# Two FFN2 chunks in the array's 64-row lanes, and two small moves in the start-up of a gated state-space and feed-forward kernel

## The chip, the cores and the metric

The kernel runs on one core of one Trainium2 chip. The metric is the device time of one execution in microseconds (us), taken as the median of several executions. The engines are called as in the profile: PE is TensorE (matmuls), PEld its weight loads, DVE is VectorE, ACT is ScalarE, POOL is GpSimd, SP is SyncE; SPq and ACTq are the places from which DMAs are issued.

## The reference

For one sequence of 2048 rows and 448 features, the output mixes two branches with a gate per row:

```python
g = sigmoid((x * gate_w).sum(-1, keepdims=True))
# a: a diagonal complex state-space model (P = D = 448)
Bu = x @ B_bar.T                       # B_bar from Lambda, log_dt, B
h[t] = Lam_bar * h[t-1] + Bu[t]        # 2048 steps
a = 2 * real(h @ C.T) + x * Dskip
# b: a feed-forward network, w1 448x1792 (FFN1), w2 1792x448 (FFN2)
b = silu(x @ w1) @ w2
out = g * a + (1 - g) * b
```

All inputs and the output are bf16.

## The kernel before

The rows are split into even and odd ones, 1024 each, so that the scan runs over pairs of rows. Each parity has two halves of 512 rows. The feed-forward branch works by chunks: chunk c holds parity `c // 2` and half `c % 2`. Of one chunk, FFN1 makes 14 blocks of 128 hidden features by 512 rows, two blocks at a time; ACT applies silu from PSUM and writes them to the SBUF tile `AT[c % 2]`. FFN2 of the chunk then makes four output tiles of 128 rows by 448 features, each a sum over the 14 hidden blocks in one PSUM bank, and a result step scales the bank and writes it to SBUF. For chunk 0 that step is on DVE (L790), for the others on ACT (L795).

The contraction of FFN1 is 448 = 3.5 x 128 rows. To waste none of the array, FFN1 and the products with B run in **lanes** (L358 to L396): the array's upper and lower 64 rows (`LO`, `UP`) work as two arrays of 64 x 128, each with its own weights and its own bank. `pair` sends blocks e and o through `lanes` in three passes: the first three 128-row blocks with e's lower half and o's upper half, the remainder of 64 rows for both, and a **swapped** pass that gives each bank its other half. The swapped pass is put into `waiting` and is issued by `settle()` after the next pair's first pass, so that PE need not wait: `T.passed("pe", c)` makes PE wait for its own earlier pass before the other lane adds to the same bank. FFN2 (`ffn2`, L770 to L796), the transposes of x and the last stage use the whole array of 128 rows; the last stage multiplies the states by C (L1004), called the output stage here.

All engines run in order. A small tracker (`T.op`) writes the waits from the names that an operation reads and writes. The order of the work is the order in which lines 1057 to 1182 call the pieces; several are generators that `run(g, n)` moves on by n steps: `s0` to `s3` are the scans on DVE, `t0` to `t3` the sine and cosine tables on ACT, `g0` to `g3` the gate and the skip term, `ca` and `cd` the matrices from C on ACT and DVE. PSUM has eight banks. `nxt()` hands out the next one of the list `BANKS`, `skip(n)` passes over n of them, `at(p)` names the pair of banks number p counted from `base`. FFN2 of chunk 0 is at L1102 to L1112, that of chunk 1 at L1136 to L1144; each is followed by FFN1 of the chunk after the next (chunk 2 at L1116, chunk 3 at L1149). FFN2 of chunks 2 and 3 (L1150 to L1164) is not touched.

In the start-up, x of chunk 0 is loaded in pieces (`XH`; the last piece, half of the columns, is `XA[4]`) and transposed on PE (`turn_x`, L487), two transposes for each call; DVE copies them out (`turned_x`, L495). The first six FFN1 blocks (`ffn1_first`, L425) run on the whole array, spread between the transposes by `yield`: six matmuls for each 128-row block j of the contraction. Three parameter rows (`log_dt`, `Lambda_re`, `Lambda_im`) are loaded into `R` (`ld_row`, L261), filled up to 512 columns by a small DVE copy (`rd`, L463), turned into columns by four small matmuls (`mm_cols`, L467) and copied to `PV` by DVE (L513). The transposes of blocks 1 and 3 use the same PSUM bank as these columns, so those of block 3 wait for the copy to `PV`.

Of the kernel before, what the change touches and what calls it, by code (L numbers as in the profile page):

```python
# [19 lines left out]
D = 448  # L20
F_FF = 1792
NFB = 14
# [128 lines left out]
def gated_mix(nc, A_x, A_Lambda_re, A_Lambda_im, A_B_re, A_B_im, A_C_re, A_C_im, A_log_dt,  # L151
              A_Dskip, B_x, B_w1, B_w2, gate_w, out):
    with ExitStack() as ctx:
        E = ctx.enter_context
        T = Tracker(nc, ctx)

        def sb(name, shape, dtype):
            return E(nc.sbuf_tensor(name, list(shape), dtype))
# [6 lines left out]
        W2 = sb("W2", [128, NFB, D], BF16)  # L165
# [11 lines left out]
        AT = [sb(f"AT{i}", [128, NFB, 512], BF16) for i in range(2)]  # L177
# [30 lines left out]
        def bsk(tile):  # L208
            if tile % 2:
                return BTK if tile == 1 else []  # L210
            return {0: ["IOTA"], 8: ["COS0"], 12: ["SIN0"]}.get(tile, [])
# [9 lines left out]
        ps = E(nc.psum_tensor("ps", [128, 8, 512], F32))  # L221
        BANKS = list(range(8))


        def ld(eng, dst, src, key, group=None):
            return T.dma(eng, lambda e: e.dma_start(dst, src), writes=[key], group=group)
# [23 lines left out]
        def row(v):  # L250
            return v.rearrange("(o n) -> o n", o=1)

        XH = XN[:, 0:8 * D].rearrange("p (k c) -> p k c", k=4)
        XA = ["XA0", "XA1", "XA2", "XA3", "XB"]
        FA, FB = 768, 1280
        x0 = x2[0:512, 0:512].rearrange("(k p) c -> p k c", p=128)

        def ld_w(eng, j, f0=0, f1=FA, key=""):
            ld(eng, W1E[:, j, f0:f1], B_w1[j * 128:(j + 1) * 128, f0:f1], f"W1Ej{j}{key}")

        def ld_row(eng, i, v):  # L261
            ld(eng, R[i:i + 1, 0:D], row(v), f"R{i}", gR if i < 2 else gR2)
# [5 lines left out]
        def ld_wr(eng, c, later):  # L268
            p = slice(64 * c, 64 * c + 64)
            if later:  # L270
                return ld(eng, W1E[p, 3, 384:896].rearrange("p (n f) -> p n f", n=2),
                          B_w1[384:448, FA:].rearrange("p (n c f) -> p n c f", n=2, c=2)[:, :, c, :], f"W1Es{c}")
            return ld(eng, W1E[p, 3, 0:384], B_w1[384:448, 384 * c:384 * c + 384], f"W1Er{c}")
# [5 lines left out]
        for k, eng in ((2, "sp"), (3, "act")):  # L279
            ld(eng, XH[:, k, 0:256], x0[:, k, 0:256], XA[k])  # L280
        ld_w("sp", 1)
        ld("act", XH[:, :, 256:512], x0[:, :, 256:512], XA[4])
        for i, (eng, v) in enumerate((("sp", A_log_dt), ("sp", A_Lambda_re), ("act", A_Lambda_im))):
            ld_row(eng, i, v)
        ld_w("sp", 2)
        gE = [ld_wr(eng, c, False) for c, eng in enumerate(("sp", "act"))]
        ld_w3("sp", 0, 2, FA, FB, "d")
# [21 lines left out]
        for i, src in enumerate((A_B_re, A_B_im)):  # L309
# [15 lines left out]
            base=0, channel_multiplier=1), reads=["ID"], writes=["ID"])  # L325
        T.op("pool", lambda e: e.iota(IOTA[:, :].bitcast(I32), pattern=[[1, NK]], base=0, channel_multiplier=0),
             writes=["IOTA"])
# [7 lines left out]
        n_bank = [0]  # L335

        def nxt():
            n_bank[0] += 1
            return BANKS[(n_bank[0] - 1) % len(BANKS)]

        LO, UP = slice(0, 64), slice(64, 128)
# [10 lines left out]
        def settle():  # L352
            while waiting:
                b, after = waiting.pop(0)
                b()
                after()
# [41 lines left out]
        def ff(fb):  # L398
            i, c = fb // 2, fb % 2
            return i + 3 * c if i < 3 else i + 3 + 2 * c if i < 5 else i + 5 + 2 * c  # L400
# [12 lines left out]
        base = [0]  # L413

        def at(p):
            return [BANKS[(base[0] + 2 * p + i) % len(BANKS)] for i in range(2)]
# [8 lines left out]
        def ffn1_first():  # L425
            banks = [nxt() for _ in range(NF1)]
            for j, h in ((0, 0), (0, 1), (1, None), (2, None)):
                c = slice(0, 512) if h is None else slice(256 * h, 256 * h + 256)
                for n, fb in enumerate((0, 2, 4, 1, 3, 5)):
                    bank = banks[fb]  # L430
                    T.op("pe", lambda pe, fb=fb, bank=bank, j=j, h=h, c=c: pe.matmul(  # L431
                        ps[:, bank, c], W1E[:, j, ff(fb) * 128:(ff(fb) + 1) * 128], XT[:, j, c],
                        start=(h == 0), stop=(h == 0), skip_group_check=(h != 0)),
                        reads=[f"W1Ej{j}" if j else f"W1Ej0{fb % 2}"] + (
                            ["XTe02"] if j == 2 else [f"XTe0{j}{h}"] if h is not None else [f"XTe0{j}0", f"XTe0{j}1"]),
                        writes=[f"ps{bank}"])
                    if (j, h, n) in ((0, 0, 3), (0, 0, 5), (1, None, 2)):
                        yield
            yield banks

# [46 lines left out]
        def turn_x(j, i):  # L487
            def mm(pe):
                ins = None
                for k in (2 * i, 2 * i + 1):  # L490
                    ins = pe.transpose(xp[j][:, k * 128:(k + 1) * 128], XH[:, k, j * 128:(j + 1) * 128], ID[:, :])  # L491
                return ins
            T.op("pe", mm, reads=(XA[2 * i:2 * i + 2] if j < 2 else [XA[4]]) + ["ID"], writes=[f"ps{PB[j]}"])

        def turned_x(j, i=None):  # L495
            c, key = (slice(0, 512), f"XTe0{j}") if i is None else (slice(256 * i, 256 * i + 256), f"XTe0{j}{i}")
            T.op("dve", lambda e: e.tensor_copy(XT[:, j, c], xp[j][:, c]), reads=[f"ps{PB[j]}"], writes=[key])

        for j in range(2):
# [3 lines left out]
        first = ffn1_first()  # L503
# [9 lines left out]
        T.op("dve", lambda e: e.tensor_copy(  # L513
            PV[:, :, :], ps[:, 7, 256:288].rearrange("p (t c) -> p t c", c=8)[:, :, 0:4]),
            reads=["pv", "ps7"], writes=["PV"])
        for j in (2, 3):
            for i in range(2):
                turn_x(j, i)
        turned_x(2)

        names = {}

# [21 lines left out]
        def pact(o, a, f, ra, scale=1.0, bias=0.0):  # L544
# [20 lines left out]
            reads=["f2"] + SGN, writes=["f2s"])  # L565
        first = next(first)
# [59 lines left out]
        def block(tile):  # L626
            return tile // 4 if tile > 7 else tile % 2
# [10 lines left out]
        def skip():  # L638
            for b in range(4):
                v, ks = xblock(b)  # L640
                T.op("dve", lambda e, v=v: e.tensor_tensor(
                    v, v, DB[:, :].unsqueeze(1).to_broadcast([128, 4, D]), ALU.mult),
                    reads=ks + ["DB"], writes=[f"XD{b}"] + ks)
                yield
# [12 lines left out]
             writes=["BTz"] + BTK[2:4])  # L657
# [7 lines left out]
        W2K = ["W20", "W21"]  # L665
# [95 lines left out]
        def xd(tile):  # L761
            return XN[:, tile * D:(tile + 1) * D]
# [5 lines left out]
                 reads=[f"XD{block(tile)}", "GRO"], writes=[f"ps{bank}"])  # L768

        def ffn2(c, q):  # L770
            odd, h = c // 2, c % 2
            kt = 4 * h + q
            tile = 2 * kt + odd
            a = AT[c % 2]
            first = c != 2
            settle()
            bank = nxt()

            def mm(pe):
                ins = None  # L780
                for fb in range(NFB):
                    ins = pe.matmul(ps[:, bank, 0:D], a[:, fb, q * 128:(q + 1) * 128], W2[:, ff(fb), :],  # L782
                                    start=(first and fb == 0), stop=(fb == NFB - 1),
                                    skip_group_check=not first)
                return ins
            T.op("pe", mm, reads=[f"AT{c % 2}_{fb}" for fb in range(NFB)] + W2K,
                 writes=[f"ps{bank}"])
            ks = [f"BS{tile}"] + bsk(tile)
            if c == 0:
                T.op("dve", lambda e: e.scalar_tensor_tensor(  # L790
                    bs(tile), ps[:, bank, 0:D], GT[:, 3, tile:tile + 1], xd(tile), ALU.mult, ALU.add),
                    reads=[f"ps{bank}", "GRI", f"XD{block(tile)}"], writes=ks)
                return
            sc = GT[:, 3, tile:tile + 1] if h == 0 else GT[:, 2, tile:tile + 1]
            T.op("act", lambda e: e.activation(bs(tile), ps[:, bank, 0:D], AF.Copy, scale=sc),  # L795
                 reads=[f"ps{bank}", "GT2" if h else "GRI"], writes=ks)  # L796
# [213 lines left out]
        def yopen():  # L1010
            return yhalf(YA, *seeds.pop(0))
# [30 lines left out]
        def run(g, n=10 ** 9):  # L1042
            for _ in range(n):
                if next(g, "end") == "end":
                    break

        coef = side_coef()
        ca, cd = c_act(), c_dve()
# [50 lines left out]
        settle()  # L1099
        run(g3, 1)  # L1100
        run(s1, 1)
        n_bank[0] = base[0] + 6  # L1102
        run(g1)
        ffn2(0, 0)
        run(s0, 1)
        ffn2(0, 1)
        run(t3)
        run(g2, 4)
        ffn2(0, 2)
        run(g2)  # L1110
        run(g3)
        ffn2(0, 3)  # L1112
        run(s0, 1)
        run(s3, 1)
        run(g0)
        f = ffn1(2)  # L1116
# [16 lines left out]
        run(s0)  # L1133
        run(s3)
        run(s1, 5)
        ffn2(1, 0)  # L1136
        run(t2)
        ffn2(1, 1)
        run(ca, 4)
        skip(4)  # L1140
        ffn2(1, 2)
        run(ca)
        ffn2(1, 3)
        skip(2)  # L1144
        run(cd)
        run(s2, 2)
        run(s1)
# [17 lines left out]
        for _ in range(8):  # L1165
            t = yclose(*yopen())
# [4 lines left out]
        kt, odd = tiles[-1]  # L1171
# [6 lines left out]
        for c in (slice(0, 280), slice(280, D)):  # L1178
            kt, odd, bank = seeds.pop(0)
# [37 lines left out]
```

## Time and profile before

| | |
|---|---|
| median of 3 runs | 137.66 us (137.56 to 137.89) |
| the profiled execution | 137.38 us |
| its span, first to last instruction | 136.1 us |
| PE busy | 133.1 us, 98% of the span |
| DVE busy | 113.9 us, 84% |
| ACT busy | 93.9 us, 69% |
| granted TensorE clock | 1.000 |

The page lists the busy time of each engine, the chain of work that ended last (followed back from the last instruction), and the costliest groups of instructions by line. The timeline lists instructions in order of time; neighbours of the same line, engine and shape are merged into one row with their count, and the length of a row reaches to the end of its last instruction. A matmul's own length (some 0.35 to 0.38 us here) includes the way through the array, and the next one starts before it ends; the rate is read from the starts. Times are us from the start of the span unless marked ns. A few matmul records are missing from the trace.

### The profile page before, as it was taken

Reading aid. Unit: us, or ns where it says so; the run is one execution under the profiler, and the core shown is the slowest. Engines: PE = TensorE matmul, PEld = TensorE weight load, DVE = VectorE, ACT = ScalarE, POOL = GpSimd, SP = SyncE. Lnnn points to the kernel's source line nnn. Section 1 sums busy time; section 2 is a strip of 40 time slices with the busy share of each in tenths; the row PEclk is TensorE's granted clock in tenths of the full one; section 3 lists DMA queues with packets and bytes.
Section 4 is the critical chain, followed back from the end, with each engine's and each line's share of the span. In section 5 each row is a group of like instructions: output and inputs, shape, how many; then the busy total and the mean of one; then the engine's idle time right before and its main releaser. Section 6 shows DMA issues by size and latency. Waiting matters only on the chain.

```text
span 136.1 us, 2407 instructions
## 1 busy us (share of the span) xinstructions
PE 133.1 (98%) x962; PEld 66.3 (49%) x963; DVE 113.9 (84%) x150; ACT 93.9 (69%) x146; POOL 16.9 (12%) x32
## 2 busy tenths in 40 slices
PE   7999999999999999999999999999999999999993
PEld 7744444444444554444445544445555555555552
DVE  1377999375699999999999999999999999991554
ACT  0458888899939999778996996797213436879300
POOL 7109669314000000000000000000000000000000
PEclk9999999999999999999999999999999999999999
DMA  4998949999999230000311000000000000222123
GB/s 111 261 288 163 161 99 169 183 145 367 299 205 198 55 92 0 5 0 0 76 43 39 0 0 0 0 5 0 0 0 0 0 5 0 101 84 85 67 79 124
DMA packets 24911, 11.94 MB, mean 88 GB/s; under 512 B 16579, under 2 KB 24390, under 8 KB 24902
## 3 DMA queue, kind: packets, MB, share of 16 engines
q1 hardware_dynamic: 23156, 10.76, 35.4%
q10 hardware_dynamic: 1746, 1.04, 2.7%
q8 instruction: 7, 0.11, 0.3%
q14 instruction: 2, 0.02, 0.0%
HBM read 5.51 MB, written 1.84 MB: 54 GB/s over the span
## 4 chain that ended last, share of the span: by engine, by line
PE 97%; DVE 1%; issue 0%
PE ps L363 43%; PE ps L782 31%; PE ps L1004 15%; PE ps L431 4%; PE ps L479 2%; PE ps L491 1%; DVE TMPS L1028 1%; PE ps L445 1%; PE ps L470 0%
## 5 line engine op out<-in xcount | busy, mean ns | idle before, releaser
L782 PE MATMUL ps<-W,AT 128*128 128x448 bf16 x224 | 42.9, 353 | 0.0
L363 PE MATMUL ps<-XT,W1E 64*128 64x512 bf16 x325 | 41.4, 376 | 0.0
L453 ACT ACTIVATE AT<-ps 128x1024 bf16<-128x1024 f32 x28 | 28.2, 1019 | 8.1 <-PE ps L363 7.6
L782 PEld LDWEIGHTS ps<-W,AT 128*128 128x128 bf16 x224 | 21.7, 98 | 21.2 <-ACT CO L733 0.4
L363 PEld LDWEIGHTS ps<-XT,W1E 64*128 64x128 bf16 x325 | 16.7, 94 | 19.4 <-issue 0.4
L363 PE MATMUL ps<-XT,BT 64*128 64x512 bf16 x156 | 22.4, 376 | 0.0
L795 ACT ACTIVATE BT<-ps,GT 128x448 bf16<-128x448 f32 x8 | 5.1, 633 | 13.2 <-PE ps L782 13.2
L363 PEld LDWEIGHTS ps<-XT,BT 64*128 64x128 bf16 x156 | 8.1, 94 | 9.3 <-DVE HS L851 0.3
L895 DVE TENSOR_TENSOR_SCAN G<-P,Q 128x1024 f32<-128x1024 f32 (+1 forms) x6 | 11.4, 1920 | 0.0
L1004 PE MATMUL ps<-CO,VE 128*128 128x448 bf16 (+2 forms) x63 | 11.1, 332 | 0.0
L1004 PE MATMUL ps<-CO,HS 128*128 128x448 bf16 x56 | 11.1, 352 | 0.0
L851 DVE SCALAR_TENSOR_TENSOR HS<-VE,P,ps 128x512 bf16<-128x512 bf16 (+1 forms) x13 | 9.6, 779 | 1.7 <-PE ps L363 1.6
L363 PE MATMUL ps<-XR,W1E 64*128 64x512 bf16 x25 | 9.2, 376 | 0.0
L1004 PEld LDWEIGHTS ps<-CO,VE 128*128 128x128 bf16 x63 | 6.0, 98 | 4.8
L1004 PEld LDWEIGHTS ps<-CO,HS 128*128 128x128 bf16 x56 | 5.5, 98 | 5.1
L848 DVE TENSOR_TENSOR Q<-G,COS 128x2048 bf16<-128x2048 f32 (+1 forms) x4 | 7.0, 1756 | 0.1
L848 DVE TENSOR_TENSOR Q<-G,SIN 128x2048 bf16<-128x2048 f32 (+1 forms) x4 | 7.0, 1750 | 0.0
L813 ACT ACTIVATE VE<-ps 128x1024 bf16<-128x1024 f32 x6 | 6.1, 1019 | 1.2 <-PE ps L363 1.2
L815 ACT ACTIVATE ps<-VE,P 128x1024 f32<-128x1024 bf16 x6 | 6.7, 1118 | 0.2
L851 DVE SCALAR_TENSOR_TENSOR VE<-HS,P,FP 128x512 bf16<-128x512 bf16 (+1 forms) x7 | 6.6, 977 | 0.1
L1028 DVE SCALAR_TENSOR_TENSOR OT<-ps,GT,BT 128x448 bf16<-128x448 f32 x4 | 2.6, 681 | 4.7 <-PE ps L1004 4.7
L851 DVE SCALAR_TENSOR_TENSOR FP<-HS,P,VE 128x1024 f32<-128x1024 bf16 (+1 forms) x4 | 6.2, 1550 | 0.1
(120 smaller groups left out, 173.8 us busy)
## 6 DMA issues: line engine op xcount, KB each, us to landing
W<-in_B_w_dram SPq DMA_DIRECT2D x2, 784.0 KB, 8.1
XN<-in_A_x_dram SPq DMA_DIRECT2D x1, 896.0 KB, 6.5
out_dram<-OT SPq DMA_DIRECT2D x8, 112.0 KB, 1.7
out_dram<-TMPS SPq DMA_DIRECT2D x7, 112.0 KB, 1.7
HS<-HS SPq DMA_DIRECT2D x4, 128.0 KB, 2.5
W1E<-in_B_w_dram SPq DMA_DIRECT2D x2, 192.0 KB, 4.0
XN<-in_A_x_dram SPq DMA_DIRECT2D x1, 384.0 KB, 5.8
XN<-in_A_x_dram ACTq DMA_DIRECT2D x1, 256.0 KB, 4.6
```

What stands on the lines that cost most here:

```text
L363: ins = pe.matmul(ps[:, bank, :], w(p, j), xh(odd, h, j, p), start=start and j == js[0], stop=stop and j == js[-1], skip_group_check=seeded)
L431: T.op("pe", lambda pe, fb=fb, bank=bank, j=j, h=h, c=c: pe.matmul(ps[:, bank, c], W1E[:, j, ff(fb) * 128:(ff(fb) + 1) * 128], XT[:, j, c] ...
L453: T.op("act", lambda e: e.activation(a[:, fb:fb + n, :], ps[:, bank:bank + n, :], AF.Silu), reads=[f"ps{bank + i}" for i in range(n)], wri ...
L782: ins = pe.matmul(ps[:, bank, 0:D], a[:, fb, q * 128:(q + 1) * 128], W2[:, ff(fb), :], start=(first and fb == 0), stop=(fb == NFB - 1), sk ...
L795: T.op("act", lambda e: e.activation(bs(tile), ps[:, bank, 0:D], AF.Copy, scale=sc), reads=[f"ps{bank}", "GT2" if h else "GRI"], writes=ks)
L813: T.op("act", lambda e: e.activation(VE[:, m:m + 2, hs], ps[:, b[0]:b[0] + 2, :], AF.Copy), reads=[f"ps{i}" for i in b], writes=vs)
L815: T.op("act", lambda e: e.activation(ps[:, o[0]:o[0] + 2, :], VE[:, m:m + 2, hs], AF.Copy, scale=c1("lr", pt)), reads=vs + ["lr"], writes= ...
L848: T.op("dve", lambda e: e.tensor_tensor(o, a, b, op), reads=reads, writes=writes)
L851: T.op("dve", lambda e: e.scalar_tensor_tensor(o, a, s, b, ALU.mult, ALU.add), reads=reads, writes=writes)
L895: T.op("dve", lambda e: e.tensor_tensor_scan(G[:, c, w], rb, Q1[:, c, w], init, ALU.mult, ALU.add), reads=[f"Q1{c}", "rr", f"G{c}"], write ...
L1004: ins = pe.matmul(ps[:, bank, c], state(kt, odd, m), CO[:, m, c], start=False, stop=(m == YB[-1]), skip_group_check=True)
L1028: T.op("dve", lambda e: e.scalar_tensor_tensor(o, ps[:, bank, c], g, bs(tile)[:, c], ALU.mult, ALU.add), reads=[f"ps{bank}", "GT1_1", f"BS ...
```

## The change

Three edits.

1. FFN2 of chunks 0 and 1 no longer uses the whole array. `ffn2_all(c)` takes the four tiles as two couples. `ffn2_lanes` runs one pass of 14 x 2 matmuls of 64 rows by 448 columns: the lower lane adds to one tile's bank, the upper lane to the other's. First the first pass of both couples, then the swapped pass of both; before a swapped pass PE waits for the end of the same couple's first pass. The result steps move into `ffn2_out`, unchanged in themselves, and are called in two groups of two. So the order on DVE (chunk 0) and on ACT (chunk 1) changes: the second scan step comes ahead of chunk 0's first result, and table `t2` and three steps of `ca` come ahead of chunk 1's first two results. For chunk 0 the bank list is rearranged.
2. The DMA of the third parameter row (`Lambda_im`, on ACT's queue) is issued before the last piece of x instead of after it.
3. The first six FFN1 blocks get a further `yield`, and the three matmuls before it are put between the transposes of x's block 2 and those of block 3.

```diff
@@ loads
-        ld("act", XH[:, :, 256:512], x0[:, :, 256:512], XA[4])
         for i, (eng, v) in enumerate((("sp", A_log_dt), ("sp", A_Lambda_re), ("act", A_Lambda_im))):
             ld_row(eng, i, v)
+        ld("act", XH[:, :, 256:512], x0[:, :, 256:512], XA[4])
@@ ffn1_first
-                    if (j, h, n) in ((0, 0, 3), (0, 0, 5), (1, None, 2)):
+                    if (j, h, n) in ((0, 0, 3), (0, 0, 5), (1, None, 2), (1, None, 5)):
                         yield
@@ start-up
-        for j in (2, 3):
-            for i in range(2):
-                turn_x(j, i)
+        for i in range(2):
+            turn_x(2, i)
         turned_x(2)
+        next(first)
+        for i in range(2):
+            turn_x(3, i)
@@ new functions
+        def ffn2_lanes(c, lo, up, start):
+            a = AT[c % 2]
+
+            def mm(pe):
+                ins = None
+                for fb in range(NFB):
+                    for p, (q, bank) in ((LO, lo), (UP, up)):
+                        ins = pe.matmul(ps[:, bank, 0:D], a[p, fb, q * 128:(q + 1) * 128], W2[p, ff(fb), :],
+                                        start=(start and fb == 0), stop=(not start and fb == NFB - 1))
+                return ins
+            T.op("pe", mm, reads=[f"AT{c % 2}_{fb}" for fb in range(NFB)] + W2K,
+                 writes=[f"ps{lo[1]}", f"ps{up[1]}"])
+            return T.count["pe"]
+
+        def ffn2_all(c, apart=0):
+            settle()
+            two = []
+            for q in (0, 2):
+                two.append([(q, nxt()), (q + 1, nxt())])
+                skip(0 if q else apart)
+            cs = [ffn2_lanes(c, *t, True) for t in two]
+            for k, t in zip(cs, two):
+                T.passed("pe", k)
+                ffn2_lanes(c, t[1], t[0], False)
+            return [lambda t=t: ffn2_out(c, *t) for t in two[0] + two[1]]
@@ chunk 0
-        n_bank[0] = base[0] + 6
+        BANKS[:] = at(3) + at(2) + at(0) + at(1)
+        n_bank[0] = 0
         run(g1)
-        ffn2(0, 0)
+        outs2 = ffn2_all(0)
         run(s0, 1)
-        ffn2(0, 1)
         run(t3)
         run(g2, 4)
-        ffn2(0, 2)
+        for o in outs2[0:2]:
+            o()
         run(g2)
         run(g3)
-        ffn2(0, 3)
+        for o in outs2[2:4]:
+            o()
         run(s0, 1)
@@ chunk 1
-        ffn2(1, 0)
+        outs2 = ffn2_all(1, 4)
+        skip(2)
         run(t2)
-        ffn2(1, 1)
-        run(ca, 4)
-        skip(4)
-        ffn2(1, 2)
+        run(ca, 3)
+        for o in outs2[0:2]:
+            o()
         run(ca)
-        ffn2(1, 3)
-        skip(2)
+        for o in outs2[2:4]:
+            o()
         run(cd)
```

More of the change, by code (lines that the diff above doesn't have):

```diff
@@ L770, in ffn2 @@
         def ffn2(c, q):
[L771 to L775, printed above, removed]
             settle()
-            bank = nxt()
+            bank, a, first = nxt(), AT[c % 2], c != 2
             def mm(pe):
@@ L787, in ffn2, with ffn2_out @@
                  writes=[f"ps{bank}"])
+            ffn2_out(c, q, bank)
+        def ffn2_lanes(c, lo, up, start):
[21 more added lines that the diff above has]
+            return [lambda t=t: ffn2_out(c, *t) for t in two[0] + two[1]]
+        def ffn2_out(c, q, bank):
+            odd, h = c // 2, c % 2
+            tile = 2 * (4 * h + q) + odd
             ks = [f"BS{tile}"] + bsk(tile)
```

## The prediction

> **What bounds the kernel now.** I read the page first: busy times and the chain that ended last.
>
> ```profile
> PE 133.1 (98%) x962; PEld 66.3 (49%) x963; DVE 113.9 (84%) x150; ACT 93.9 (69%) x146; POOL 16.9 (12%) x32
> ...
> PE 97%; DVE 1%; issue 0%
> ```
>
> PE is the chain: 97% of the span is PE following itself, from 0.82 us to the last matmul at 133.8. Behind that lie only the last result steps on DVE, their DMAs, and 137.38 - 136.1 = 1.28 us outside the span, none of which the change touches. So a microsecond is won only where PE's own timeline gets shorter, and lost wherever PE is made to wait. The granted clock is 1.000. What is left to win on PE is seen in its timeline, from the starts of the rows:
>
> ```profile
> 41.91 0.81 PE L363 MATMUL ps<-XT,W1E 64*128 64x512 bf16 x6
> 42.66 10.77 PE L782 MATMUL ps<-W,AT 128*128 128x448 bf16 x56
> 53.36 0.82 PE L363 MATMUL ps<-XT,W1E 64*128 64x512 bf16 x6
> 54.02 0.38 PE L363 MATMUL ps<-XR,W1E 64*128 64x512 bf16 x1
> ...
> 69.34 0.81 PE L363 MATMUL ps<-XT,BT 64*128 64x512 bf16 x6
> 70.08 10.77 PE L782 MATMUL ps<-W,AT 128*128 128x448 bf16 x56
> 80.78 0.82 PE L363 MATMUL ps<-XT,W1E 64*128 64x512 bf16 x6
> 81.44 0.38 PE L363 MATMUL ps<-XR,W1E 64*128 64x512 bf16 x1
> ...
> 112.66 5.46 PE L1004 MATMUL ps<-CO,HS 128*128 128x448 bf16 x28
> 117.96 1.11 PE L1004 MATMUL ps<-CO,VE 128*128 128x448 bf16 x5
> ```
>
> Lane passes of three pairs follow one another every 0.647 us elsewhere (22.24, 22.89; 24.40, 25.05), 0.2158 for a pair. A pass that starts at 41.91 would hand over at 42.56; FFN2 starts at 42.66, 0.10 later. Full-array matmuls of 448 columns run at (117.96 - 112.66) / 28 = 0.1892 us, so FFN2's 56 should take 10.60, to 53.26; the lanes start at 53.36, again 0.10 late. Chunk 1 shows the same two edges (69.99 against 70.08, 80.68 against 80.78). FFN2 to the output stage, both on the whole array, shows none: 112.28 plus two matmuls is 112.66, though PE waits there for DVE's states. Nor do the waits between lane passes cost anything. So each edge is the price of going from lanes to the whole array or back, 0.10 us plus about 0.01 in the first interval behind it.
>
> Then the start-up, PE and DVE:
>
> ```profile
> 7.36 0.24 PE L470 MATMUL ps<-ID,R 128*128 128x4 bf16 x4
> 7.46 0.81 PE L491 MATMUL ps<-ID,XN 128*128 128x128 bf16 x8
> 8.32 1.89 PE L431 MATMUL ps<-XT,W1E 128*128 128x512 bf16 x8
> ```
>
> ```profile
> 6.98 0.17 DVE L464 COPY R<-R 3x64 bf16<-3x64 bf16 x1 [0.77 <-DMA R<-in_A_Lambda_im_dram]
> 7.64 0.17 DVE L513 COPY PV<-ps 128x16 f32<-128x16 f32 x1 [0.49 <-PE ps L470]
> 7.88 0.42 DVE L497 COPY XT<-ps 128x512 bf16<-128x512 bf16 x1
> 8.23 0.15 DVE L549 SCALAR_TENSOR_TENSOR P<-PV,P 128x4 f32<-128x4 f32 x1
> 8.30 0.16 DVE L542 TENSOR_TENSOR P<-P,PV 128x4 f32<-128x4 f32 x1
> 8.37 0.42 DVE L497 COPY XT<-ps 128x512 bf16<-128x512 bf16 x1
> 8.82 0.42 DVE L554 COPY XR<-ps 64x512 bf16<-64x512 bf16 x1
> ```
>
> Eight transposes at 0.055 would last from 7.46 to 7.90. Four are done at 7.68; the fifth waits for the copy to PV (ends 7.82) and starts at 7.87 (the waits name 0.2 us of L491 behind L513). The row of 8 at 8.32 should hold 9; the weight loads list 9, so the first started at 8.11. PE stands still for 0.19 us.
>
> **Lanes for FFN2.** The work becomes 56 pairs of 64-row matmuls per chunk instead of 56 matmuls of 128 rows. No row shows a pair with 448 columns. Both nearest rows give the same overhead over the columns: the output stage's last tile, cut in 280 and 168 columns, starts its matmuls every 0.119 and 0.0725 us, 0.418 ns a column, so 0.2158 less 64 columns is 0.189; a matmul of 448 columns has 0.1892. I take 0.1892. The lower end is 0.2158 x 448/512 = 0.1888, the upper end 0.2158, if something other than columns paces pairs. Against the upper end: a pair brings two loads and two matmuls, four instructions in 0.189, and the 168-column matmuls bring two in 0.0725, a denser stream. Against loads as a bound: the loads of a pair start 4 ns apart and last 0.094, inside 0.189.
>
> The Trainium skill, "TensorE: Matmul & The Clock Gate" (Part 3, The mechanism), says that a weight load overlaps a running matmul only in another row group; in lanes the next load goes to a lane that is still busy, and by that rule an estimate would be 112 x 0.094 = 10.5 us more. The trace differs: lane pairs keep 0.2158 a pair with such loads in every one, where that rule would make it 0.31.
>
> Chunk 0: pass at 41.91, FFN2 from 42.56, 56 x 0.1892 = 10.60, then the first pass of chunk 2 (0.65) ends at 53.80 instead of 54.02. Gain 0.21. Chunk 1: 69.34 + 0.65 + 10.60 + 0.65 = 81.23 instead of 81.44. Gain 0.21. The edge before chunk 2's FFN2 at 91.5 stays.
>
> The added waits of PE on itself: a swapped pass waits for a pass that ended 14 pairs, 2.65 us, before; FFN1's swapped passes do so with less room and no gap. Behind each stands the whole rest of PE's queue, but the waits are met.
>
> Banks of chunk 0: its second couple starts at 42.37 + 2.65 = 45.0 and takes the pair that scan s1's first step on DVE reads, done at 42.75. From FFN1 of chunk 2 on, banks come round in the old rhythm, four pairs later.
>
> **Later results.** Chunk 0: the third pass ends near 50.5, the fourth near 53.1. DVE does the second scan (2.28) first, ends it near 51.6, two results until 52.8, waits for the fourth pass, two results from 53.2 to 54.4; in the row of before this point is 54.07. So the whole DVE queue behind (s0, s3, s1, cd, s2) is 0.3 late. Its cover: the last states that PE waits for, HS of s2, are done at 120.30 and used near 125.9; 5.6 us. Banks of the results: freed by 54.4, wanted at 55.3 and 56.8. Cost nothing; without that cover 0.3.
>
> Chunk 1, on ACT: t2 and three steps of ca need 3.2 + 1.95 us from about 71.25 on, so ACT is free at 76.4 and waits for the third pass until 77.7. Behind that wait are two results (1.05), four steps of ca (2.25), two results (1.14, done 82.2), then silu of chunk 3, due at 82.55. PE wants those last two banks for chunk 3's third pair at 82.34. The cover is 0.1 us, and a load more (0.1) before a matmul is late. I take nothing; if ACT is one ca step late, 0.3 to 0.4 goes.
>
> **Start-up.** With three matmuls (0.647) behind the fourth transpose: 7.68 + 0.65 = 8.33, four transposes to 8.55, then block 2's six matmuls, which started at 8.755. Gain 0.20. Their own wait, DVE's copy of block 2, ends at 8.31. Late next: block 3's copies on DVE, 8.75 to 9.62 instead of 8.37 to 9.24; PE wants them near 9.94 (10.14 before). The DVE and POOL chain to the first table is 0.38 later and has until the idle stretch of DVE at 25 to 27 us.
>
> The row sooner: DVE's first small copy can go 0.5 us earlier, but mm_cols started at 7.36, the moment the matmul before it (7.145 + 0.216) let go, so PE gains nothing. The last piece of x is issued later by one row issue: 0.22 to 0.37 (SP's two rows) or 0.64 (ACT's own, start to next start). It was issued at 2.20 and landed 4.6 later, at 6.80; PE wants it at 7.44. At worst 7.44 plus a release, a stall of 0.05; I take 0.37 and none. The small row in front of it on that queue adds to no other: SP's order is the same, and ACT's later loads keep their place.
>
> **Sum.** 0.20 + 0.21 + 0.21 = 0.62. On the profiled execution 137.38 - 0.62 = 136.76; that execution is 0.28 below the median, so the median goes from 137.66 to 137.04.
>
> **The rivals.** About 0.3%, 0.41 us here, is what a measurement of this kernel can tell from no change.
> - The edges are not the switch of the array. All four also carry a wait on ACT or DVE. If these waits were the gaps, only the start-up is won: 137.46. Against it: waits of the same kind inside lanes and at 112.66 cost nothing. 7%.
> - Gains are given back by one wait: ACT's last results of chunk 1 (0.3 to 0.4), or the start-up's 0.20 lost to the last piece of x or block 3's copies: 137.2 to 137.55. For it speaks the 0.1 of cover. 13%.
> - Slower: the pair's pace. If a pair of FFN2 takes longer than 0.1892, all 112 pay. At 0.1947 the 0.62 are eaten, from 0.1984 on the kernel is slower by over 0.41; at the upper end 0.2158 it is 112 x 0.0266 = 2.98 more, 140.0. For it: no such pair is in the trace, and twice the weight loads are asked of PE for the same columns. Against it: the two pace rows above. 12%.
>
> **How the numbers follow.** The forecast has 68%, its own range 136.9 to 137.2 (0.1 for the median, 0.05 for x's last piece). 80% needs the give-back and the edge rival, up to 137.55, and leaves the slow pair out; at the lower end 136.8, if pairs run at 0.1888 and the median strays. Faster by over 0.3% (below 137.25): the forecast and the mild end of the give-back, 0.70. Within: the edge rival and the rest, 0.17. Slower: 0.13.
>
> **What would show it.** Right: the timeline has 448-column rows of 64x448 x112 without a gap at either side, 10.6 us long, chunk 3's first pass 0.6 earlier than 80.78, no idle of L491 behind L513, the output stage starting near 112.05. Wrong: pairs of more than 0.1892, a gap at 42.4 or 53.1, PE idle near 82.3 behind L795 or near 7.4 behind the last piece of x.

## The result, and the profile after

| | before | after |
|---|---|---|
| median | 137.65 us (21 runs) | 136.97 us (21 runs) |
| ratio, 95% interval | | 0.995 [0.9929, 0.9971] |
| the profiled execution | 137.38 us, span 136.1 | 137.75 us, span 135.9 |

The median fell by 0.68 us; 0.62 was forecast. The interval of the ratio means 0.40 to 0.98 us. The profiled execution of after is not a typical one: it lies 0.78 us above its own median, 0.57 of that outside the span (137.75 - 135.9 = 1.85, against 1.28 in the execution of before). Executions of one kernel differ by more than the change does, so the trace has to be read piece by piece. First the page, busy times and the chain that ended last:

```profile
PE 132.5 (98%) x1074; PEld 66.5 (49%) x1075; DVE 114.0 (84%) x150; ACT 93.7 (69%) x146; POOL 16.9 (12%) x32
...
PE 92%; DMA 4%; ACTq 1%; DVE 1%; issue 0%
```

PE has 112 more matmuls and is busy 0.6 us less. The chain has a piece that was not in it before: 4% DMA, the load of x. The timeline of PE around FFN2 of both chunks and into the output stage (start, length, instruction):

```profile
42.12 0.81 PE L363 MATMUL ps<-XT,W1E 64*128 64x512 bf16 x6
42.77 10.76 PE L794 MATMUL ps<-W,AT 64*128 64x448 bf16 x112
53.36 0.81 PE L363 MATMUL ps<-XT,W1E 64*128 64x512 bf16 x6
54.01 0.38 PE L363 MATMUL ps<-XR,W1E 64*128 64x512 bf16 x1
...
69.33 0.81 PE L363 MATMUL ps<-XT,BT 64*128 64x512 bf16 x6
69.98 10.76 PE L794 MATMUL ps<-W,AT 64*128 64x448 bf16 x112
80.58 0.81 PE L363 MATMUL ps<-XT,W1E 64*128 64x512 bf16 x6
81.22 0.38 PE L363 MATMUL ps<-XR,W1E 64*128 64x512 bf16 x1
...
112.44 5.46 PE L1032 MATMUL ps<-CO,HS 128*128 128x448 bf16 x28
```

From 42.12 every piece follows without a gap: 0.65, 10.59 (56 pairs at 0.1892), 0.65. From the last pass before FFN2 to the end of the first pass behind it are 11.89 us, 12.11 before; chunk 1 has 11.89 against 12.10. That is 0.22 + 0.21, as forecast. But the last output matmul started at 133.58 instead of 133.80, only 0.22 earlier. The other 0.2 went in the start-up, of which this is PE and DVE:

```profile
7.23 0.24 PE L470 MATMUL ps<-ID,R 128*128 128x4 bf16 x4
7.85 0.40 PE L491 MATMUL ps<-ID,XN 128*128 128x128 bf16 x4 [0.38 <-DMA XN<-in_A_x_dram]
8.30 0.59 PE L431 MATMUL ps<-XT,W1E 128*128 128x512 bf16 x2
8.73 0.39 PE L491 MATMUL ps<-ID,XN 128*128 128x128 bf16 x4
8.96 1.46 PE L431 MATMUL ps<-XT,W1E 128*128 128x512 bf16 x6
10.35 0.39 PE L445 MATMUL ps<-XT,W1E 64*128 64x512 bf16 x1
```

```profile
7.51 0.17 DVE L513 COPY PV<-ps 128x16 f32<-128x16 f32 x1 [1.06 <-PE ps L470]
8.29 0.42 DVE L497 COPY XT<-ps 128x512 bf16<-128x512 bf16 x1 [0.61 <-PE ps L491]
9.16 0.42 DVE L497 COPY XT<-ps 128x512 bf16<-128x512 bf16 x1 [0.30 <-PE ps L491]
9.62 0.42 DVE L556 COPY XR<-ps 64x512 bf16<-64x512 bf16 x1
```

The transposes of block 3 (8.73) no longer wait for PV, and the three matmuls stand before them (two of the three are recorded). But the transposes of block 2 start at 7.85 instead of 7.33, where the small matmuls end: they wait for x's last piece, which landed at 7.81, 6.80 before. The first remainder (L445) starts at 10.35 instead of 10.14. So of the signs that the prediction named, this trace shows both kinds: 64x448 x112 without a gap and no idle behind L513, but chunk 3's first pass only 0.20 earlier, the output stage at 112.44 instead of 112.05, and PE idle behind the last piece of x, which was to be a sign of being wrong. In the third execution of the changed kernel that was profiled (after_third, below) the same two places are at 79.96 and 111.83, 0.82 and 0.83 earlier than before.

The result steps moved as worked out. On DVE the second pair of chunk 0 waits 0.52 for the fourth pass; on ACT the first pair of chunk 1 waits 1.35:

```profile
51.80 1.25 DVE L818 SCALAR_TENSOR_TENSOR IOTA<-ps,GT,XN 128x448 bf16<-128x448 f32 x2
53.57 1.28 DVE L818 SCALAR_TENSOR_TENSOR IOTA<-ps,GT,XN 128x448 bf16<-128x448 f32 x2 [0.52 <-PE ps L794]
54.77 2.28 DVE L876 TENSOR_TENSOR Q<-G,COS 128x2048 bf16<-128x2048 f32 x1
```

```profile
78.13 1.16 ACT L823 ACTIVATE COS<-ps,GT 128x448 bf16<-128x448 f32 x2 [1.35 <-PE ps L794]
79.18 0.67 ACT L715 ACTIVATE FP<-XC,P 128x448 f32<-128x448 bf16 x1
79.74 1.78 ACT L715 ACTIVATE TMPS<-XC,P 128x448 f32<-128x448 bf16 x3
81.42 1.15 ACT L823 ACTIVATE SIN<-ps,GT 128x448 bf16<-128x448 f32 x2
```

Neither reaches PE: the banks that ACT gives back at 82.57 (81.42 + 1.15) are wanted at 82.74, by chunk 3's third pair.

### The profile page after: what moved, and what is told of

Read it like the earlier page. It is cut to its first block, busy times and chain, and to the rows that moved or that the text cites. A ratio compares the mean times of both kernels' runs of the same rounds, so it can differ in the third digit from the quotient of the medians.

```text
span 135.9 us, 2631 instructions
## 1 busy us (share of the span) xinstructions
PE 132.5 (98%) x1074; PEld 66.5 (49%) x1075; DVE 114.0 (84%) x150; ACT 93.7 (69%) x146; POOL 16.9 (12%) x32
## 3 DMA queue, kind: packets, MB, share of 16 engines
q1 hardware_dynamic: 23156, 10.76, 33.7%
## 4 chain that ended last, share of the span: by engine, by line
PE 92%; DMA 4%; ACTq 1%; DVE 1%; issue 0%
PE ps L363 43%; PE ps L779 16%; PE ps L794 16%; PE ps L1032 15%; DMA XN<-in_A_x_dram 4%; PE ps L431 1%; ACTq L226 1%; DVE TMPS L1056 1%; PE ps L445 1%; PE ps L491 0%
## 5 line engine op out<-in xcount | busy, mean ns | idle before, releaser
L453 ACT ACTIVATE AT<-ps 128x1024 bf16<-128x1024 f32 x28 | 28.2, 1018 | 7.4 <-PE ps L363 7.2
L794 PE MATMUL ps<-W,AT 64*128 64x448 bf16 x224 | 21.5, 349 | 0.0
L779 PE MATMUL ps<-W,AT 128*128 128x448 bf16 x112 | 21.4, 353 | 0.0
L794 PEld LDWEIGHTS ps<-W,AT 64*128 64x128 bf16 x224 | 10.9, 94 | 10.4
L779 PEld LDWEIGHTS ps<-W,AT 128*128 128x128 bf16 x112 | 10.9, 98 | 10.5 <-issue 0.4
```

What stands on the lines that cost most here:

```text
L453: T.op("act", lambda e: e.activation(a[:, fb:fb + n, :], ps[:, bank:bank + n, :], AF.Silu), reads=[f"ps{bank + i}" for i in range(n)], wri ...
L794: ins = pe.matmul(ps[:, bank, 0:D], a[p, fb, q * 128:(q + 1) * 128], W2[p, ff(fb), :], start=(start and fb == 0), stop=(not start and fb = ...
```

## The experiments

The theory to be tested: an edge between lanes and whole array costs 0.105 us of PE, the four removed edges are 0.42, and the rest comes from the start-up, by when x's last piece and the third row land. The rivals: the gaps at the edges were waits, or the start-up brings everything. In what follows two times of the trace divide the kernel: the start of the first remainder, L445, up to which the start-up decides, and the start of the last output matmul. The span was taken of every execution too, and leaves out the time outside it; where mean spans are compared, the figure behind ± is two standard errors.

**Lanes alone.** Edits 2 and 3 are undone in the changed kernel:

```diff
+        ld("act", XH[:, :, 256:512], x0[:, :, 256:512], XA[4])
         for i, (eng, v) in enumerate((("sp", A_log_dt), ...
-        ld("act", XH[:, :, 256:512], x0[:, :, 256:512], XA[4])
...
-        next(first)
```

> FFN2 of chunks 0 and 1 in lanes; the start-up as before (no row sooner, transposes not moved). Theory: each edge between lanes and whole array costs 0.105 us, so the four edges are the whole gain here: 0.42 us less than before, 137.2; in the profile 448-column pairs start every 0.1895 us and the passes on both sides join without a gap, the last piece of x is in time as before and the first remainder (L445) starts near 10.15. Rival (the gaps at the edges were waits on ACT or DVE, and the whole gain came from the start-up): no change, 137.6.

Measured: 137.24 us median against 137.42, ratio 1.0001 [0.9974, 1.0029]. The interval holds no change and leaves 0.42 (0.9969) just outside; the mean span is 0.16 ± 0.26 us shorter, with 0.42 at its edge. So the times don't show the gain. The trace shows it behind the start-up: from L445 (10.26) to the last output matmul (133.49) are 123.22 us, in the trace of before 123.65: the 0.42. The start-up was 0.12 later than in the trace of before, and not for the reason that I knew:

```profile
6.26 0.82 PE L431 MATMUL ps<-XT,W1E 128*128 128x512 bf16 x3 [0.15 <-DMA W1E<-in_B_w_dram]
7.48 0.24 PE L470 MATMUL ps<-ID,R 128*128 128x4 bf16 x4 [0.40 <-DVE R L464]
7.58 0.81 PE L491 MATMUL ps<-ID,XN 128*128 128x128 bf16 x8
```

Here the small matmuls wait 0.40 for the third row (landed at 7.08), a wait that the trace of before does not have.

**Twice the edges.** One couple in lanes, the other two tiles on the whole array, each behind a lane pass (`ffn2_whole` is the matmul loop of before for one tile); start-up as before:

```diff
-            cs = [ffn2_lanes(c, *t, True) for t in two]
-            for k, t in zip(cs, two):
-                T.passed("pe", k)
-                ffn2_lanes(c, t[1], t[0], False)
+            lo, up = two[0]
+            k = ffn2_lanes(c, lo, up, True)
+            ffn2_whole(c, *two[1][0])
+            T.passed("pe", k)
+            ffn2_lanes(c, up, lo, False)
+            ffn2_whole(c, *two[1][1])
```

> FFN2 of chunks 0 and 1 with twice as many edges as before: one couple in lanes, the other two tiles on the whole array, one behind each lane pass; results in the changed kernel's order, the start-up as before. Theory (an edge costs 0.105 us whichever work stands at it): four gaps of about 0.10 in each chunk, so from the first L445 to the last output matmul 123.65 + 0.42 = 124.07 us, 0.85 more than with FFN2 in lanes alone (123.22); a time 0.3% over before. Rival (the gaps of before were waits on ACT or DVE at the chunk's two ends): 123.65 or less, since only the inner edges without such waits are new.

Measured: 138.18 us against 137.81, ratio 1.0025 [0.9993, 1.0057]; L445 to the last output matmul 124.07 us, as expected to the digit. The ratio alone is unclear; the spans of the ten executions are 0.46 ± 0.22 us longer than before's, where 0.42 was expected. PE in chunk 0:

```profile
42.10 0.81 PE L363 MATMUL ps<-XT,W1E 64*128 64x512 bf16 x6
42.75 2.81 PE L792 MATMUL ps<-W,AT 64*128 64x448 bf16 x28
45.49 2.82 PE L805 MATMUL ps<-W,AT 128*128 128x448 bf16 x14
48.25 2.82 PE L792 MATMUL ps<-W,AT 64*128 64x448 bf16 x28
51.00 2.82 PE L805 MATMUL ps<-W,AT 128*128 128x448 bf16 x14
53.76 0.82 PE L363 MATMUL ps<-XT,W1E 64*128 64x512 bf16 x6
```

From lanes into lanes (42.10, 42.75) 0.65, no gap. Each FFN2 piece of 14 steps should take 2.65 and takes 2.74 to 2.76: four gaps where before had two. In chunk 0 the profile names no wait at any of the four, and from the start of the last matmul ahead of an edge to the first behind it the interval is over the pace by 0.092 to 0.096, at these edges as at those of before, after and lanes_only, L431 to L445 in the start-up among them. The gap belongs to the switch, wherever it stands; the rival of the waits is out.

What PE does in the gap is not settled. Inside one form the next weight load starts 2 to 4 ns behind the start of the matmul ahead of it and is covered by it. At the edge of before into chunk 0's FFN2 the last lane matmul starts at 42.351, and the first load only at 42.655, with its matmul at 42.660. The gap is as long as a load takes (0.094 to 0.098), so it may be a load that nothing covers, or an array that has to empty; no run separates the two.

**The start-up edits without lanes**, both, and each alone (the same lines as in the change):

> The two start-up edits without lanes. Theory: between 0.20 faster and 0.35 slower than before, by when x's last piece lands: issued 0.5 us later than before it lands between 7.1 and 7.8, and every 0.1 us behind 7.4 is PE idle in front of L491. Rival (the start-up brings what the changed kernel has over 0.42): 0.26 faster.

Measured: 137.09 us against 137.42, ratio 0.9975 [0.9951, 1.0000]. In the trace the last piece landed at 7.76, L491 waited for it and L445 came at 10.30: this trace speaks for the loss, the ratio for the gain. On the same chip the changed kernel has 137.06 (below): by the times the start-up edits alone do as well as with the lanes, and the mean spans differ by 0.01 ± 0.34. Here too the 0.42 of the lanes is in the traces and not in the times.

> Only the third parameter row ahead of x's last piece. Theory (the row sooner makes x's last piece land 0.8 to 1.0 us later and PE waits for it): row lands near 4.2, last piece 7.7 to 7.8, PE idle 0.4 to 0.6 us in front of L491, first L445 at 10.35 to 10.4 against 10.15 to 10.26 before: same to 0.2 slower. Rival (the row sooner is the gain of the start-up): 0.2 to 0.3 faster, L445 near 9.9.

Measured: 137.09 us against 137.81, ratio 0.9962 [0.9934, 0.9990]. The expectation failed. Row at 4.16, but last piece at 6.81, no idle before it, and L445 at 9.62, the rival's side:

```profile
6.17 0.82 PE L431 MATMUL ps<-XT,W1E 128*128 128x512 bf16 x3 [0.23 <-DMA W1E<-in_B_w_dram]
6.83 0.24 PE L470 MATMUL ps<-ID,R 128*128 128x4 bf16 x4
6.93 0.81 PE L491 MATMUL ps<-ID,XN 128*128 128x128 bf16 x8
7.79 1.89 PE L431 MATMUL ps<-XT,W1E 128*128 128x512 bf16 x8
9.62 0.39 PE L445 MATMUL ps<-XT,W1E 64*128 64x512 bf16 x1
```

L445 is 0.52 earlier than in the trace of before, yet chunk 0's FFN2 starts at 42.72, 0.06 later: all of that start was lost again, at 32.9 us:

```profile
32.08 0.38 PE L363 MATMUL ps<-XT,BT 64*128 64x512 bf16 x1
32.90 1.25 PE L363 MATMUL ps<-XT,BT 64*128 64x512 bf16 x10 [0.45 <-DVE HS L851]
```

```profile
31.12 0.29 DVE L238 COPY XR<-XT 64x512 bf16<-64x512 bf16 x1 [1.47 <-DMA XT<-in_A_x_dram]
31.44 1.41 DVE L851 SCALAR_TENSOR_TENSOR HS<-VE,P,ps 128x512 bf16<-128x512 bf16 x2
```

DVE's copy of x's last remainder (L238) waits for its DMA until 31.1; behind it in DVE's queue stands the scan's first step, which frees the bank that PE wants. PE, early, finds it at the time when it would have found it anyway. So this trace does not show where the ratio's gain came from; its span (136.2) is 0.4 over the median span of the twelve executions (135.8). Nor is the landing at 4.16 of the third row what lets the small copy (L464) go: it starts at 6.27, behind the two rows on SP's queue, which landed at 6.24. Against 6.98 in the trace of before, edit 2 brings that copy forward by 0.7 us.

> Only the moved transposes, no lanes, no row sooner. Theory: no idle of L491 behind L513, first L445 0.2 to 0.3 earlier than before (near 9.9); from there to the last output matmul 123.65 as before, unless DVE's copy of x's last remainder (L238) is held by its DMA at 31 us; 0.2 less than before. Rival (the start-up is set by the DMAs whatever PE's order): L445 at 10.15 or later, same.

Measured: 137.51 us against 137.62, ratio 0.9987 [0.9967, 1.0006]; L445 at 9.83, then 123.65 us to the last output matmul, as the theory has it. The mean span is 0.25 ± 0.17 us shorter.

**Lanes and transposes, the row as before.** Only edit 2 is undone in the changed kernel.

> Lanes and the moved transposes, but the third parameter row behind the last piece of x as before. Theory: the row sooner is worth nothing and its delay of x's last piece is what made PE idle 0.54 us at 7.3 in the profile of the changed kernel; without it the last piece lands near 6.8, L491 has no idle, L445 starts near 9.94: 0.62 us less than before, and 0 to 0.4 less than the changed kernel. Rival (the row sooner is part of the gain, since in many executions the row is late behind the last piece): 0.42 less than before or worse, slower than the changed kernel by 0.2 or more, with mm_cols (L470) late.

Measured: 137.12 us against 137.42, ratio 0.9993 [0.9967, 1.0020]. In the trace L445 came at 9.91 and the last output matmul at 133.13, 0.66 before that of the kernel before; yet this execution took 137.12 us, with 1.69 outside the span. The times put it behind the changed kernel (137.12 against 137.06 on that chip), the spans ahead (medians 135.55 and 135.75): eight of its twelve executions had over 1.5 us outside the span, four of the changed kernel's. Not settled.

**The changed kernel again**, twice, each beside others on one chip:

> The changed kernel once more beside the others. Theory: 0.4 to 0.7 us less than before; in its profile x's last piece is issued near 2.75 and lands between 7.1 and 7.8, with PE idle in front of L491 between 0 and 0.5 us. Rival (the idle in the first profile was an accident of that execution): landing near 6.9 and no idle.

> The changed kernel a third time, on the chip of the others. Theory: 0.3 to 0.7 less than before; x's last piece between 6.8 and 7.8, PE idle in front of L491 where it lands behind 7.2; 123.22 us from the first L445 to the last output matmul where the copy L238 is not late. Rival (lanes bring nothing and the first comparison was luck): same time as before.

Measured: 137.06 us against 137.42, ratio 0.9974 [0.9944, 1.0004], last piece at 7.69, L445 at 10.23; and 136.99 against 137.62, ratio 0.9967 [0.9942, 0.9991], last piece at 7.20, L445 at 9.74, 123.22 us from there to the last output matmul at 132.96. With the first comparison these are 0.68, 0.36 and 0.63 us of the medians; 0.36 is less than the theory's 0.4. The first of the two traces is of the longest of its twelve executions (138.31 us): PE stood 0.67 for the last piece, and lost 0.74 more between L445 and FFN2, at 33.7, as row_only did at 32.9.

**Other loads for the start-up.** The third row from SP, with x's last piece where it was; and x's last piece in two loads, row between them:

```diff
+        ld("act", XH[:, :, 256:512], x0[:, :, 256:512], XA[4])
-        for i, (eng, v) in enumerate((("sp", A_log_dt), ("sp", A_Lambda_re), ("act", A_Lambda_im))):
+        for i, (eng, v) in enumerate((("sp", A_log_dt), ("sp", A_Lambda_re), ("sp", A_Lambda_im))):
             ld_row(eng, i, v)
-        ld("act", XH[:, :, 256:512], x0[:, :, 256:512], XA[4])
```

```diff
...
+        ld("act", XH[:, :, 256:384], x0[:, :, 256:384], XA[4])
         for i, (eng, v) in enumerate((("sp", A_log_dt), ("sp", A_Lambda_re), ("act", A_Lambda_im))):
             ld_row(eng, i, v)
-        ld("act", XH[:, :, 256:512], x0[:, :, 256:512], XA[4])
+        ld("act", XH[:, :, 384:512], x0[:, :, 384:512], XA[5])
```

> Lanes, moved transposes, the third row issued by SP right behind the other two, x's last piece on ACT where it was before. Theory: row near 6.3, last piece 6.8 to 7.15, block 2 of w1 0.2 later (7.7 to 7.9, wanted near 8.4); no idle in front of L491 or L470, first L445 at 9.6 to 9.9: 0.6 to 0.8 less than before, 0.2 to 0.4 less than the changed kernel. Rival (the last piece is late whatever stands ahead of it): L445 near 10.3 and no better than the changed kernel.

> The changed kernel with x's last piece in two loads by columns: block 2 first, then the third row, then block 3. Theory: block 2 (half the bytes) lands near 6.5, the row near 6.7, block 3 7.3 to 7.7 where PE wants it at 8.2; no idle in front of L491, L445 at 9.6 to 9.9: 0.6 to 0.8 less than before. Rival (rows of 256 bytes cost the queue as much as those of 512): block 2 near 6.8, block 3 behind 8.2, L445 at 10.0 or later.

Measured: 137.60 us (0.9995 [0.9967, 1.0024]) and 138.02 us (1.0017 [0.9988, 1.0046]) against 137.81. The rows on SP landed at 7.03 and 7.26, not 6.3, and L445 came at 10.25: a miss. The split did for the start what was expected (block 2 at 6.17, row 6.37, L445 at 9.35, early) and lost it all later: by the starts of its matmuls PE stood still for 1.27 us until 28.8, behind a DMA transpose of x that landed at 28.72 (25.8 to 26.7 in the other traces but xr_after), and for 0.38 until 33.7, behind DVE's scan step.

**The later copy.** To free the scan's first step from that DMA, `swap_xr("dve", 1, 1)` is put behind it, with the row sooner and without:

```diff
-        swap_xr("dve", 1, 1)
         pair(*bu3_even(0, 0))
...
         run(s0, 1)
+        swap_xr("dve", 1, 1)
         bu_odd(0, 1)
```

> The changed kernel with one more edit: DVE's copy of x's last remainder (L238, second half, odd rows) behind the scan's first step instead of before it. Theory (in some executions the DMA in front of that copy lands so late that the copy holds the scan's first step, and the bank that PE wants at 32.7 with it: idle of 0.6 to 0.8 us in three of ten traces so far): no gap on PE near 32.7 in this trace whenever the DMA lands, 32.4 us from the first L445 to chunk 0's FFN2; on the average of executions 0.1 to 0.3 less than the changed kernel, and fewer slow ones. Rival (that wait is only found where the start-up was early anyway, and something else then ends last): a new gap behind it, no gain.

> Lanes, moved transposes, row behind x's last piece as before, and the same later copy. Theory: L445 near 9.9 and 32.4 us from it to chunk 0's FFN2: 0.6 to 0.9 less than before, the best of all versions. Rival: no better than the changed kernel.

Measured: 137.82 us (0.9993 [0.9959, 1.0027]) and 137.44 us (0.9995 [0.9978, 1.0011]) against 137.62. The rival was right: PE now waits for the copy itself, in both.

```profile
31.18 1.46 PE L363 MATMUL ps<-XT,BT 64*128 64x512 bf16 x12
33.04 0.39 PE L363 MATMUL ps<-XR,BT 64*128 64x512 bf16 x1 [0.40 <-DVE XR L238]
```

PE wants that copy at 32.5 and 32.3, and behind the scan's first step it comes too late. In the first of the two the start-up was the earliest of all (last piece 6.72, L445 at 9.26, 0.88 before the trace of before); 0.75 of it went at 28.2, behind a DMA transpose of x that landed at 28.11, and the rest and more at 33.0: FFN2 starts at 42.98, 0.32 later than before.

## Why the prediction was right, point by point

**The lanes: right in mechanism and size, by the traces.** 0.42 was forecast. The time from the start of chunk 0's FFN2 to the last output matmul is 91.13 to 91.14 us in the four traces with the whole array and 90.80 to 90.81 in the nine with lanes (four_edges, with both, has 91.65); the first edge adds 0.10 in front of it. Sum 0.42, the same in every trace. A pair of 448 columns takes 0.1892, the value taken from the two pace rows; the upper end and with it the slower rival are out. The entry of FFN2 still carries a wait on ACT in the changed kernel and costs nothing, and four_edges shows four gaps: the edge rival is out too. What the traces show, the times of whole executions have not confirmed: lanes_only gained 0.16 ± 0.26 of the span, and the changed kernel nothing over start_both on the same chip. Why is open; in the nine traces with lanes nothing behind the start of FFN2 took the 0.42 back.

**The covers held.** DVE came 0.70 later to the scan's next step (54.77 against 54.07; 0.3 was forecast, with FFN2 starting at 42.37, and it started at 42.77), hidden. ACT's last results had 0.17 to spare where 0.1 was worked out.

**The start-up: the number about right, the steps partly wrong.** The transposes' 0.20 hold where the last piece is in time: from the small matmuls (L470) to L445 are 2.78 to 2.79 us with neither edit or with the row alone (before, lanes_only, four_edges, row_only) and 2.58 to 2.59 with the transposes moved (turns_only, lanes_turns, xr_turns, rows_sp). Two steps failed. The last piece of x was to land at 7.44 at worst; I added the later issue (measured 0.56: the row took 0.53 of ACT's queue) to the landing of before, and it landed at 7.81, 1.01 later; with the same order of issue it landed anywhere from 6.72 to 7.81. And the row sooner was to gain nothing, since in the trace of before the small matmuls started the moment PE was free. That holds for one execution. In others PE came sooner and waited for the row (0.40 in lanes_only). Over the traces L445 starts at 10.14 to 10.33 with neither edit (before, lanes_only, four_edges), 9.82 to 9.91 with the transposes alone (turns_only, lanes_turns, xr_turns), 9.62 with the row alone, and at 9.26, 9.74, 10.23, 10.30 and 10.35 with both (xr_after, after_third, after_again, start_both, after). The mean of the last five is 9.98, 0.27 before the first three. The row sooner cuts both ways: the small matmuls start at 6.65 to 7.23 (mean of six traces 6.95) instead of 7.24 to 7.54 (mean of six 7.37), and behind them PE then stands for up to 0.67 us for the last piece. So the start-up brought something like the 0.2 that I had written, by a chain that I had not: which of the rows, the last piece and block 1 of w1 lands last. That the sum came out is in part luck: a gain and a loss that it left out lie near each other, and of the three comparisons of the changed kernel one, with 0.36, lies outside the 0.46 to 0.76 of the forecast's own range.

**What the forecast did not see** is the second limit at 32.7 us. In the trace of before DVE's copy L238 ends at 31.29, its DMA having landed at 30.96, the scan's first step starts at 31.38, and PE, which needs the bank of that step, comes 0.02 late. By these times all but about 0.1 us of an earlier start would have been lost there; I read over it. The DMA lands between 29.4 and 31.6 us in these traces. A start-up that gains more finds DVE's scan step late, behind that DMA (row_only) or behind the one in front of DVE's copy before it, which landed at 29.0 and 29.2 instead of the 26.5 to 27.4 of ten other traces (rows_sp, after_again). It took back 0.59 in row_only, 0.51 in rows_sp and 0.74 in after_again, which is the changed kernel itself.

What stays open: the share of each start-up edit, and of the lanes, in the mean of executions. The intervals of single kernels are 0.2 to 0.35% to either side, as wide as the effects, and each trace is one execution. In spans, lanes_only gained 0.16 ± 0.26, turns_only 0.25 ± 0.17, row_only 0.32 ± 0.25 and start_both 0.34 ± 0.25, each against before on its chip; the changed kernel gained 0.35 ± 0.28 and 0.58 ± 0.23, less than the traces' 0.42 for the lanes and the 0.34 of start_both add up to.

## What to carry to other kernels

Going between a divided and a whole array has a price that is paid per switch, not per matmul: keep neighbouring stages in one form where the column counts allow it, and read the price off the starts at the edges. A step shown free in one trace is free in that execution; where loads land with a spread of half a microsecond, ask what PE finds when it comes earlier. And look for the next place with no slack before paying for an earlier start.

## What the runs showed of the hardware

- A switch of the array between two 64-row lanes and 128 rows costs 0.095 us and about 0.01 in the next interval, at a granted clock of 1.000, in either direction. The Trainium skill, "TensorEngine Tiling (Array Packing)" (Key Properties), says that changing the mode drains the engine, without a number; these traces give the price of the edge, and do not show whether a drain is what takes it.
- PE's pace doubles at a time that differs from execution to execution: the first matmuls of 256 columns start 0.213 us apart, later 0.109, and the first short interval ends between 4.1 (lanes_only, row_only) and 6.9 us (rows_sp; 6.6 in before), after the same 22 warm-up matmuls. The granted clock reads 0.9 or more in all of it on the page. In the traces with a late change of pace, before and after among them, PE comes to the small matmuls without having waited for block 1 of w1.
- A load of one row of 896 bytes holds ACT's DMA issue for 0.53 to 0.61 us, SP's for 0.22 to 0.34, and for 0.51 where it was SP's third in a row (rows_sp). Behind the row on ACT's queue, the 256 KB of x landed 4.0 to 5.1 us after their issue.
- The time outside the span gathers at two values, near 1.27 and near 1.75 us, and the share of the longer one (over 1.5) among the kernel before's runs was 5, 22 and 10 of 35 in the three groups. It moves a median by more than some of the edits do.
